# Moving the weight sums of a two-MoE kernel: three steps per piece, other places in the order, and an earlier gather of the inputs of phase one

## Chip, cores and metric

One core of one Trainium2 chip runs the whole kernel in one launch. The metric is the device time of one execution in microseconds; for the kernel before it is 1974.27 us, the median of three runs (1972.3, 1974.27 and 1975.72).

## What is computed

A windowed attention is followed by two mixture-of-experts layers, each with 8 experts on 2304 tokens of width 512, hidden width 1024. The first MoE gives each token to one expert (288 tokens each); the second applies every expert to every token and weighs the results by a matrix P that is balanced in 8 rounds.

```python
def _moe2_ref(x, w_gate, w1, w2):
    logits = x @ w_gate
    P = np.exp(logits - logits.max())
    for _ in range(8):
        P /= P.sum(1, keepdims=True) + 1e-09
        P /= P.sum(0, keepdims=True) + 1e-09
        P *= N / E
    for e in range(E):
        out += P[:, e:e + 1] * (np.maximum(x @ w1[e], 0.0) @ w2[e])
```

## The kernel before

**Number format.** Each fp32 operand is held as two f16 parts, hi and lo, and a product is three matmuls (hi by hi, hi by lo, lo by hi).

**Stages.** Up to about 165 us the attention runs. From there to 747 us, stage 1 (`stage1`) interleaves the router of the first MoE, its eight experts in phases 0 to 7 (`moe1`, after `moe1_x` has transposed the gathered inputs), and expert 0 of the second MoE (`m2_l1(j)`, `m2_l2(j)`: layers 1 and 2 on the j-th of nine column blocks). The end of stage 1, 668.6 to 746.0 us, is `last()`: both layers on blocks 7 and 8, interleaved with a side generator `sinkhorn`, which computes the gate's logits (L1131, L1132: 18 tiles) and balances P (eight rounds, each with a matmul L1157 between two short chains of DVE operations). A side generator goes on whenever the main one has issued as many nanoseconds of matmul as the side asked for in its last `yield`. `drain=False` leaves the rest of `sinkhorn` to the next stage.

**Stage 2** (`stage2`, 747 us to the end) runs experts 1 to 7, each over three blocks of 384 token pairs (below n = 0, 1, 2). It uses Strassen's scheme: seven products of matrix halves instead of eight. `s_l1` issues 28 products (q, i) of six matmuls (L1022, 168 in all), of which `after` makes hidden values: C[i] in a tile "r" of two buffers and S[i] in a tile "S" of one. `split` turns them into f16: hh (ACT, L978) and hl (DVE, L979); its four steps per i are put off over later products by the list `todo`. `s_l2` has 84 steps and 252 matmuls (L1060); `add` sums the products (L1083 to L1093) and weighs them by P into `acc` (L1070).

**Weight sums.** For Strassen each expert's weights are seven sums and pieces of matrix quarters. They come in eight pieces p0 to p7 (four of layer 1, four of layer 2) by the generator `pieces`. For each it loads the raw fp32 weights (SP queue, L903 or L906), makes four sums (DVE, L918 to L921 or L924 to L927; below A), the hi part (ACT, two L937; B) and the lo part (DVE, two L940; C). For experts 2 to 7 both parts go to DRAM (`ws`, POOL queue, L943), and `w_load` brings back a layer's weights whole (SP queue, w1h, w1l, w2h, w2l: 1792 KB each). A piece is done in one go: A and B in one step at one of the steps j = 8, 20, 32, ... of `s_l2`, C and the stores twelve steps on. Expert 1's pieces stay in SBUF: six fall into `last()`, a step every five of its main steps, two into the first `s_l1`. The 18 rows of `acc`, which expert 0 has filled (L880), are scaled by P on POOL (L1288).

**Phase 0.** `weights(("a", 0))` gathers the weights of the first expert through the POOL queue (L768, four tiles of w1a, converted by ACT L747 and DVE); `gather_x` gathers the 288 tokens (L777, three). `moe1_x` transposes them on PE (L809, copied by ACT L810), and `moe1` multiplies (L796).

What sets the order of each engine is the order of these calls in the program; tiles with few buffers add waits.

Of the kernel before, what the change touches and what calls it, by code (L numbers as in the profile page):

```python
# [650 lines left out]
BLK = 384  # L651
# [24 lines left out]
class Moe:  # L676
# [40 lines left out]
    def weights(self, key, letter, fetch):  # L717
# [17 lines left out]
        for it in todo[:4]:  # L735
            load(it)
# [154 lines left out]
    def pieces(self, e, lay, sums, ns=range(4), stored=False):  # L891

        nc = self.nc
        V = nc.vector
        sw = (SW1, SW2)[lay]
# [13 lines left out]
        ns = list(ns)  # L909
        nxt = load(ns[0])  # L910
        yield
        for n in ns:
            r = nxt
            t = sums()
            x = [r[:, k] for k in range(4)]
            if lay == 0:
                a11, a21, a12, a22 = x
                V.tensor_add(t[:, 0], a21, a22)  # L918
                V.tensor_sub(a21, a11, a21)  # L919
                V.tensor_sub(t[:, 1], t[:, 0], a11)  # L920
                V.tensor_sub(t[:, 2], a12, t[:, 1])  # L921
            else:
                b11, b12, b21, b22 = x
                V.tensor_sub(t[:, 0], b12, b11)  # L924
                V.tensor_sub(b12, b22, b12)
                V.tensor_sub(t[:, 1], b22, t[:, 0])
                V.tensor_sub(t[:, 2], b21, t[:, 1])  # L927
            if stored:
                hi, lo = (self.raw.tile([128, 1024], F32, name="raw").bitcast(F16)[:, :7 * 256].rearrange(
                    "p (k c) -> p k c", k=7) for _ in range(2))  # L930
            else:
                hi, lo = (o[:, n] for o in self.wb[lay])
            if n != ns[-1]:
                nxt = load(ns[ns.index(n) + 1])
            parts = (slice(0, 4), r), (slice(4, 7), t)
            for k, x in parts:
                nc.scalar.activation(hi[:, k], x, AF.Copy, scale=sw)  # L937
            yield
            for k, x in parts:
                V.scalar_tensor_tensor(lo[:, k], x, sw, hi[:, k], op0=OP.mult, op1=OP.subtract)  # L940
            if stored:
                for u, x in enumerate((hi, lo)):
                    nc.gpsimd.dma_start(self.ws[lay][u, :, n], x)  # L943
            yield
# [19 lines left out]
    def s_l1(self, b):  # L964
# [16 lines left out]
        def after(q, i):  # L981
# [60 lines left out]
    def s_l2(self, e):  # L1042
# [65 lines left out]
    def load_gate2(self):  # L1108
        nc, sm = self.nc, self.sm
        g = sm.tile([128, KT, E], F32, name="g2f")  # L1110
        self.g2 = sm.tile([128, KT, 2, E], F16, name="g2")
        nc.sync.dma_start(g, self.wg2.rearrange("(k p) e -> p k e", p=128))
        nc.scalar.activation(self.g2[:, :, 0], g, AF.Copy, scale=SG)
        nc.vector.scalar_tensor_tensor(self.g2[:, :, 1], g, SG, self.g2[:, :, 0], op0=OP.mult, op1=OP.subtract)

    def sinkhorn(self):

        nc, sm = self.nc, self.sm
        V = nc.vector
        self.P = P = sm.tile([128, NT, E], F32, name="P")  # L1120
        one_f = sm.tile([128, 128], F32, name="one_p")
        V.memset(one_f, 1.0)
        p = self.r.psum()
        pv = p[:, :2 * NT * E].rearrange("p (t w e) -> p t w e", e=E, w=2)
        for t in range(NT):
            if t % 3 == 0:
                yield 600
            s, j = divmod(t, NT // 2)
            c = slice(128 * j, 128 * (j + 1))
            for k in range(KT):  # L1130
                nc.tensor.matmul(pv[:, t], self.x2[0][:, k, s, c], self.g2[:, k], start=(k == 0), stop=False)  # L1131
# [36 lines left out]
    def stage1(self, ctx):  # L1168
# [30 lines left out]
        def main():  # L1199
# [10 lines left out]
            for ph in range(E):  # L1210
# [16 lines left out]
                if ph + 1 == E:  # L1227
                    break
# [118 lines left out]
```

## Time and profile before

| what | value |
|---|---|
| median of three runs | 1974.27 us |
| profiled execution, its own time | 1982.54 us |
| its span, first to last instruction | 1980.8 us |
| mean granted TensorE clock in it | 0.961 |
| PE busy | 1805.1 us, 91% |
| DVE busy | 1409.7 us, 71% |
| ACT busy | 886.5 us, 45% |
| POOL busy | 322.5 us, 16% |

Rows of a timeline have the start in us, the duration in us, engine, line, operation, tiles written and read, shape and count; what stands in brackets at the end is how long the engine sat idle before the row, and what released it. Rows of waits have the waiting engine's tile and line, the releasing engine's tile and line, the idle time in us, how often, and the longest. PE is TensorE's matmuls, DVE VectorE, ACT ScalarE, POOL GpSimd, SP SyncE (a queue of transfers here).

### The profile page before, as it was taken

The numbers are of one execution on the slowest core, as the hardware profiler recorded it, in microseconds if no ns is written. First come the engines' busy times: TensorE is split into PE (matmuls) and PEld (weight loads), VectorE is DVE, ScalarE is ACT, GpSimd is POOL, SyncE is SP. The second block draws the span as 40 slices with busy tenths as digits, with TensorE's granted clock in tenths as the row PEclk, the third lists the DMA queues.
The fourth block names the chain that finished last, engine by engine and source line by source line (L and its number), as shares of the span: only waits on it lengthen the run. The fifth ranks groups of instructions, "written<-read, shape, count | busy, mean of one in ns | idle before, by whom it ended". The sixth has DMA issues, their size and how long they took to land.

```text
span 1980.8 us, 36661 instructions
## 1 busy us (share of the span) xinstructions
PE 1805.1 (91%) x15082; PEld 1322.0 (67%) x15082; DVE 1409.7 (71%) x2680; ACT 886.5 (45%) x1532; POOL 322.5 (16%) x377
## 2 busy tenths in 40 slices
PE   6997589998899778999999999999999999999998
PEld 4775367665667645677776667777667776766776
DVE  5996677766764377777778777677867777787655
ACT  6784233323334224443454444345544444554333
POOL 0582332222242006000000000000000000000111
PEclk7897699999999889999999999999999999999999
DMA  9275553444463231235333333443334334323220
GB/s 216 68 156 139 108 110 72 99 117 68 110 146 98 69 110 58 98 144 195 137 124 135 136 119 144 161 172 115 124 125 152 144 152 169 127 110 136 89 89 33
DMA packets 139816, 241.21 MB, mean 122 GB/s; under 512 B 74208, under 2 KB 107232, under 8 KB 132736
## 3 DMA queue, kind: packets, MB, share of 16 engines
q1 hardware_dynamic: 118384, 151.25, 23.5%
q0 software_dynamic: 20592, 87.53, 15.3%
q8 instruction: 118, 1.93, 0.4%
q14 instruction: 50, 0.41, 0.1%
q10 hardware_dynamic: 672, 0.08, 0.0%
HBM read 173.74 MB, written 61.74 MB: 119 GB/s over the span
## 4 chain that ended last, share of the span: by engine, by line
issue 49%; PE 6%; POOL 4%; DVE 3%; ACT 1%; DMA 1%; POOLq 0%; SPq 0%; ACTq 0%; DVEq 0%
PE mm L1022 4%; POOL ws L943 2%; POOL acc L1288 2%; PE mm L1060 1%; POOL out_dram L1074 1%; PE mm L877 1%; DMA raw<-in_w2b_dram 1%; DVE raw L940 1%; ACT hh L978 0%; ACT raw L937 0%; DVE hl L979 0%; DVE w1l L940 0%; DVE w2l L940 0%; DVE t L1088 0%; DVE t L1090 0%
## 5 line engine op out<-in xcount | busy, mean ns | idle before, releaser
L1022 PE MATMUL mm<-xb,w1h 128*128 128x384 f16 x2352 | 574.6, 327 | 32.1 <-DVE r L997 26.8
L1060 PE MATMUL mm<-w2h,hh 128*128 128x256 f16 x1764 | 481.4, 273 | 25.5 <-DVE t L1084 12.2
L1060 PE MATMUL mm<-w2l,hh 128*128 128x256 f16 x1764 | 481.5, 273 | 0.0
L1060 PE MATMUL mm<-w2h,hl 128*128 128x256 f16 x1764 | 481.5, 273 | 0.0
L1060 PEld LDWEIGHTS <-hh 128*128 128x128 f16 x3528 | 345.5, 98 | 74.9 <-issue 32.5
L1022 PE MATMUL mm<-xb,w1l 128*128 128x384 f16 x1176 | 384.1, 327 | 0.0
L1022 PEld LDWEIGHTS <-w1h 128*128 128x128 f16 x2352 | 230.3, 98 | 190.5 <-issue 43.7
L943 POOL DMA_DIRECT2D ws<-raw x96 | 51.9, 541 | 965.9 <-ACT raw L937 485.5
L979 DVE TENSOR_TENSOR hl<-r,hh 128x1536 f16<-128x1536 f32 x84 | 147.7, 1758 | 57.1 <-ACT hh L978 57.1
L1060 PEld LDWEIGHTS <-hl 128*128 128x128 f16 x1764 | 172.7, 98 | 20.3
L974 ACT ACTIVATE r<-mm 128x384 f32<-128x384 f32 x252 | 119.0, 481 | 111.2 <-PE mm L1022 111.2
L1022 PEld LDWEIGHTS <-w1l 128*128 128x128 f16 x1176 | 115.2, 98 | 76.4 <-issue 0.5
L978 ACT ACTIVATE hh<-r 128x1536 f16<-128x1536 f32 x84 | 124.6, 1484 | 47.3 <-DVE r L1003 45.2
L937 ACT ACTIVATE raw<-raw 128x1024 f16<-128x1024 f32 x48 | 50.7, 1057 | 203.4 <-DVE raw L919 99.5
L979 DVE TENSOR_TENSOR hl<-S,hh 128x1152 f16<-128x1152 f32 x84 | 113.9, 1356 | 34.5 <-ACT hh L978 34.5
L1070 DVE SCALAR_TENSOR_TENSOR acc<-t,P,acc 128x512 f32<-128x512 f32 x126 | 94.7, 752 | 5.1
L796 PE MATMUL mm<-xt,w1h 128*128 128x288 f16 x512 | 96.9, 289 | 1.6 <-ACT xt L810 1.6
L799 ACT ACTIVATE w1h<-mm 128x288 f16<-128x288 f32 (+1 forms) x120 | 46.9, 396 | 111.2 <-PE mm L796 103.2
L978 ACT ACTIVATE hh<-S 128x1152 f16<-128x1152 f32 x84 | 96.4, 1147 | 0.0
L796 PE MATMUL mm<-x2l,w0h 128*128 128x256 f16 x288 | 82.7, 287 | 10.2 <-DVE x2l L838 10.2
L800 DVE SCALAR_TENSOR_TENSOR w1l<-mm,w1h 128x288 f16<-128x288 f32 (+1 forms) x120 | 50.8, 435 | 49.8 <-ACT w1h L799 45.5
L985 ACT ACTIVATE mm<-mm 128x384 f32<-128x384 f32 x84 | 40.3, 479 | 102.5 <-PE mm L1022 102.5
(287 smaller groups left out, 3313.2 us busy)
## 6 DMA issues: line engine op xcount, KB each, us to landing
ws<-raw POOLq DMA_DIRECT2D x96, 448.0 KB
xb<-xw SPq DMA_DIRECT2D x30, 1344.0 KB
raw<-in_w2b_dram SPq DMA_DIRECT2D x32, 512.0 KB
raw<-in_w1b_dram SPq DMA_DIRECT2D x56, 256.0 KB
w1h<-ws SPq DMA_DIRECT2D x6, 1792.0 KB
w1l<-ws SPq DMA_DIRECT2D x6, 1792.0 KB
w2h<-ws SPq DMA_DIRECT2D x6, 1792.0 KB
w2l<-ws SPq DMA_DIRECT2D x6, 1792.0 KB
```

The costliest lines, as they stand in the source:

```text
L796: nc.tensor.matmul(p, a[:, k, 128 * f:128 * (f + 1)], rhs(k, b), start=(k == 0 and i == 0), stop=(k == KT - 1 and i == 2))
L799: nc.scalar.activation(h[0][:, f, :n], p, AF.Relu)
L800: nc.vector.scalar_tensor_tensor(h[1][:, f, :n], p, 0.0, h[0][:, f, :n], op0=OP.max, op1=OP.subtract)
L937: nc.scalar.activation(hi[:, k], x, AF.Copy, scale=sw)
L943: nc.gpsimd.dma_start(self.ws[lay][u, :, n], x)
L974: nc.scalar.activation(o, p, AF.Relu, scale=SH)
L978: yield nc.scalar.activation(hq[0][:, i, k], x, AF.Copy)
L979: yield V.tensor_sub(hq[1][:, i, k], x, hq[0][:, i, k])
L985: nc.scalar.activation(Q[i], P[i], AF.Copy)
L1022: nc.tensor.matmul(p, w[u][:, 2 * j + i // 2, k, 128 * (i % 2):128 * (i % 2 + 1)], x[:, v, r, j], start=(q in (1, 5) and j == 0 and n == 0 ...
L1060: nc.tensor.matmul(p, h[u][:, i, a, 128 * t:128 * (t + 1)], w[v][:, i, b, :], start=(q in (1, 7) and i == 0 and j == 0), stop=(q in (2, 3) ...
L1070: V.scalar_tensor_tensor(self.acc[:, r, :], x, self.P[:, r, e:e + 1], self.acc[:, r, :], op0=OP.mult, op1=OP.add)
```

## The change

- `pieces` goes. In its place `staged` makes the pieces of experts 2 to 7 in three steps: A; B with the store of hi; C with the store of lo. The lo part is written into a buffer of the tile "r" that C[i] uses. The steps stand at j = 0, 1, 3 of `s_l1` for n = 1 and 2 (p2, p5), and at j = 8, 10, 16 and 20, 23, 43 of `s_l2` (p0, p1 for n = 0; p3, p4 for n = 1; p6, p7 for n = 2). The first raw load is now issued before the first `s_l1` of an expert.
- `direct` makes expert 1's pieces in two steps each (A with B; C): its first loads at step 16 of the last phase's `moe1`, four steps at 40, 44, 52, 56, eight in `last()` at every tenth step, four in the first `s_l1` at j = 7, 13, 19, 25.
- The gate's logits are made after each phase (`gate2(ph - 1)`), two tiles at a time; four of the 18 tiles stay in `sinkhorn`. Its `yield`s become 2000, 1800 and 6000 instead of 1500, 1200 and 3600, and each round has one DVE operation less.
- `acc` is scaled by P on ACT in expert 1's `s_l2`, two rows of 512 ahead of each t's first sum; L1288 goes.
- In `s_l1` the split of the last but one i begins one product later.
- In phase 0 the first two weight gathers come before the tokens', the other two behind them.

The diff, cut to its core:

```diff
         for it in todo[:4]:          # weights()
+        (two loads, a yield, two loads)
 ...
+    def staged(self, e, part):
+        nxt = self.loader(e, 0)(0)
+        yield
+        for i, (lay, n) in enumerate(todo):
+            r = nxt
+            t, lo = part()
+            hi = self.raw.tile([128, 1024], F32, name="raw").bitcast(F16)[:, :7 * 256].rearrange(
+            self.w_sums(lay, r, t)
+            if i + 1 < len(todo):
+                nxt = self.loader(e, todo[i + 1][0])(todo[i + 1][1])
+            split = self.w_split(lay, r, t, hi, lo)
+            next(split)
+            yield
+            next(split)
+            nc.gpsimd.dma_start(self.ws[lay][0, :, n], hi)
+            yield
+            next(split, None)
+            nc.gpsimd.dma_start(self.ws[lay][1, :, n], lo)
+            yield
 ...
-                todo.extend((early, late, None, late))
+                todo.extend((None, early, late, late) if i + 2 == FT // 2 else (early, late, None, late))
 ...
             if q == 2:
+                for r in (row(t, 0), row(t, 1)) if e == 1 else ():
+                    nc.scalar.activation(self.acc[:, r, :], self.acc[:, r, :], AF.Copy, scale=self.P[:, r, 0:1])
 ...
-            yield 3600
+            yield 6000
 ...
-            V.tensor_scalar(cs, cs, float(CAP), None, op0=OP.mult)
 ...
+        self.ready = self.direct(1)
+                    if ph + 1 == E and i in (16, 40, 44, 52, 56):
+                        next(self.ready)
+                if ph:
+                    self.gate2(ph - 1)
 ...
-                    if j % 5 == 0:
-                        next(nxt, None)
+                    if j % 10 == 4 and n:
+                        next(self.ready)
+                        n -= 1
 ...
+        def part():
+            lo = self.tp.tile([128, 2, 2, BLK], F32, name="r", bufs=2).bitcast(F16).rearrange(
+            return self.tp.tile([128, 3, BLK], F32, name="S", bufs=1)[:, :, :256], lo
+        def l1(e, n, b):
+            for j, ns in enumerate(self.s_l1(b)):
+                if (e, n) == (1, 0) and j % 6 == 1 and j > 2:
+                    next(self.ready, None)
+                if n and e + 1 < E and j in (0, 1, 3):
+                    next(new)
+                yield ns
-        for t in range(NT):
-            self.nc.gpsimd.tensor_scalar(self.acc[:, t, :], self.acc[:, t, :], self.P[:, t, 0:1], None, op0=OP.mult)
 ...
-                    if j % 12 == 8:
+                    if j in (8, 10, 16, 20, 23, 43):
                         next(new, None)
```

**DVE at the end of a steady `s_l1`** (a block of stage 2; r, S, hh, hl and mm as above; L997 of before is L1032 after, L979 is L1014). Before:

```order
L993 TENSOR_TENSOR mm<-mm,t_10890 128x384
L1007 TENSOR_TENSOR S<-r,S 128x384
L979 TENSOR_TENSOR hl<-r,hh 128x1536
L997 TENSOR_TENSOR r<-mm,t_10890 128x384
L979 TENSOR_TENSOR hl<-S,hh 128x1152
```

After:

```order
L1028 TENSOR_TENSOR mm<-mm,t_13870 128x384
L1042 TENSOR_TENSOR S<-r,S 128x384
L1032 TENSOR_TENSOR r<-mm,t_13870 128x384
L1014 TENSOR_TENSOR hl<-r,hh 128x1536
L1014 TENSOR_TENSOR hl<-S,hh 128x1152
```

The sum of the last i's bank (r<-mm) now stands ahead of the lo part of C of the last but one i (hl<-r).

**SP at the change from stage 1 to stage 2** (xw: x's Strassen sums, written to DRAM; xb: one block of them read back; raw: weights). Before:

```order
L858 DMA xw_3240<-w2h 128x8x144
L858 DMA xw_3240<-w2l 128x8x144
L862 DMA xw_3240<-x2h 128x2x384 x3
L862 DMA xw_3240<-x2l 128x2x384 x3
L903 DMA raw<-in_w1b_dram 128x2x256 x8
L906 DMA raw<-in_w2b_dram 128x2x512 x2
L1165 DMA oidx<-lst 128x18x1
L953 DMA xb<-xw_3238 128x5376 x2
L906 DMA raw<-in_w2b_dram 128x2x512 x2
```

After:

```order
L903 DMA raw<-in_w1b_dram 128x2x256 x8
L861 DMA xw_3240<-w2h 128x8x144
L861 DMA xw_3240<-w2l 128x8x144
L865 DMA xw_3240<-x2h 128x2x384 x3
L865 DMA xw_3240<-x2l 128x2x384 x3
L906 DMA raw<-in_w2b_dram 128x2x512 x4
L988 DMA xb<-xw_3238 128x5376 x2
```

Expert 1's loads of layer 1 moved ahead of the last stores of xw, and all four of layer 2 ahead of the load of the first xb.

**POOL's queue in phase 0** (widx and idx: lists of gathered rows). Before:

```order
L768 DMA raw<-in_w1a_dram,widx 128x1024 x4
L777 DMA xg<-xd,idx 96x1024 x3
L768 DMA raw<-in_w2a_dram,widx 128x512 x8
```

After:

```order
L771 DMA raw<-in_w1a_dram,widx 128x1024 x2
L780 DMA xg<-xd,idx 96x1024 x3
L771 DMA raw<-in_w1a_dram,widx 128x1024 x2
L771 DMA raw<-in_w2a_dram,widx 128x512 x8
```

The three token gathers stand before the third and fourth weight gather.

## Rows read from the trace of the kernel before

**Rows 1.** The waits of PE, longest sums first: waiting tile and line, releaser; us in all, times, longest.

```profile
PE mm L1022 <- DVE r L997: 26.8, 22, 1.4
...
PE mm L1060 <- DVE t L1084: 12.2, 10, 2.4
PE mm L1060 <- DVE t L1088: 12.2, 18, 1.3
PE mm L809 <- DMA xg<-xd,idx: 11.1, 1, 11.1
...
PE mm L796 <- DVE x2l L838: 10.2, 9, 3.3
PE r L1140 <- DVE mx L1137: 9.4, 1, 9.4
```

**Rows 2.** DVE's timeline at the end of the `s_l1` that began at 1628.8 us.

```profile
1654.44 1.76 DVE L979 TENSOR_TENSOR hl<-r,hh 128x1536 f16<-128x1536 f32 x1 [0.68 <-ACT hh L978]
1656.11 0.55 DVE L997 TENSOR_TENSOR r<-mm,t 128x384 f32<-128x384 f32 x1
```

**Rows 3.** PE's timeline at the same place.

```profile
1656.71 0.49 PE L1022 MATMUL mm<-xb,w1h 128*128 128x384 f16 x2 [1.25 <-DVE r L997]
```

**Rows 4.** DVE's timeline in the `s_l2` that follows (n = 0 of expert 6): the last split, then A and C of a piece.

```profile
1664.21 1.35 DVE L979 TENSOR_TENSOR hl<-S,hh 128x1152 f16<-128x1152 f32 x1
1669.34 0.42 DVE L918 TENSOR_TENSOR S<-raw 128x256 f32<-128x256 f32 x1 [3.78 <-DMA raw<-in_w1b_dram]
...
1671.35 1.23 DVE L940 SCALAR_TENSOR_TENSOR raw<-raw 128x1024 f16<-128x1024 f32 x1 [0.33 <-ACT raw L937]
1672.49 0.95 DVE L940 SCALAR_TENSOR_TENSOR raw<-S,raw 128x768 f16<-128x768 f32 x1
```

**Rows 5.** ACT's timeline there: B of the same piece.

```profile
1670.26 1.06 ACT L937 ACTIVATE raw<-raw 128x1024 f16<-128x1024 f32 x1 [6.70 <-DVE raw L919]
1671.22 0.83 ACT L937 ACTIVATE raw<-S 128x768 f16<-128x768 f32 x1
```

**Rows 6.** Line 1060 in two blocks: a block of expert 7, which has no pieces, and the block of rows 4. Duration in ns (least, median, most), first and last start in us.

```profile
L1060 PE MATMUL mm<-w2h,hh x84: 272/273/273, 1832.2 to 1859.4; 128*128 128x256 f16 x84
```

```profile
L1060 PE MATMUL mm<-w2h,hh x84: 269/273/273, 1657.7 to 1687.7; 128*128 128x256 f16 x84
```

**Rows 7.** The chain that ended last, by time, in the last block (n = 2) of expert 6: start, us, what.

```profile
1774.91 12.96 DMA raw<-in_w2b_dram
```

**Rows 8.** PE's timeline in `last()`: its four long gaps; and the longest gap of the first `s_l1` of stage 2.

```profile
687.67 0.37 PE L1140 MATMUL r<-idf,mx 128*1 128x128 f32 x1 [9.41 <-DVE mx L1137]
...
705.59 0.85 PE L1157 MATMUL r<-P,one_p 128*128 128x144 f32 x2 [6.00 <-DVE P L1154]
...
719.14 0.48 PE L1157 MATMUL r<-P,one_p 128*128 128x144 f32 x2 [2.24 <-DVE P L1154]
...
727.54 0.48 PE L1157 MATMUL r<-P,one_p 128*128 128x144 f32 x2 [4.03 <-DVE P L1154]
...
771.51 0.48 PE L1022 MATMUL mm<-xb,w1h 128*128 128x384 f16 x2 [3.12 <-DVE mm L993]
```

**Rows 9.** Stretches of `last()`: from and to, us, busy us (instructions) of PE, PEld, DVE, ACT and POOL, granted clock, DMA share, GB/s.

```profile
668.60:746.00 77.40, 54.91 (x454) 36.55 (x452) 49.39 (x141) 18.95 (x36) 2.19 (x2) 0.87 0.37 114
680.40:690.70 10.30, 2.93 (x13) 1.73 (x13) 6.56 (x15) 4.78 (x9) 0.00 (x0) 0.50 0.31 99
704.30:711.20 6.90, 5.61 (x26) 4.09 (x27) 6.49 (x20) 0.74 (x3) 0.00 (x0) 0.51 0.41 79
728.20:731.60 3.40, 3.40 (x10) 1.18 (x8) 2.07 (x9) 0.00 (x0) 0.00 (x0) 0.51 0.00 0
```

**Rows 10.** SP's timeline in `last()`: loads of raw weights and of the first xb (the duration covers the issue of all transfers of the row).

```profile
676.46 17.58 SPq L903 DMA_DIRECT2D raw<-in_w1b_dram  x8
...
715.64 0.81 SPq L953 DMA_DIRECT2D xb<-xw  x2
```

**Rows 11.** DVE's timeline where it waits for the first of them.

```profile
681.30 0.42 DVE L918 TENSOR_TENSOR raw<-raw 128x256 f32<-128x256 f32 x1 [9.58 <-DMA raw<-in_w1b_dram]
```

**Rows 12.** PE's timeline: the first three gate tiles of `sinkhorn` and what follows them (24 matmuls, three tiles, up to the second row).

```profile
669.58 0.17 PE L1131 MATMUL r<-g,x2h 128*128 128x16 f16 x1
...
670.18 0.27 PE L796 MATMUL mm<-x2h,w0h 128*128 128x256 f16 x1
```

**Rows 13.** Line 880, ACT's copy of a 512-wide row of `acc`: ns, first and last start.

```profile
L880 ACT ACTIVATE acc<-mm x18: 597/597/617, 297.4 to 746.0; 128x512 f32<-128x512 f32 x18
```

**Rows 14.** ACT's timeline in phase 0: the conversion of the fourth weight tile, then the copies of the transposed tokens.

```profile
232.99 1.06 ACT L747 ACTIVATE w1h<-raw 128x1024 f16<-128x1024 f32 x1 [6.57 <-DMA raw<-in_w1a_dram,widx]
234.31 1.73 ACT L810 ACTIVATE xt<-mm 128x768 f16<-128x768 f16 x2 [0.27 <-PE mm L809]
```

**Rows 15.** POOL's timeline: one store of weight sums (448 KB), whose bytes rows 16 show as they move.

```profile
1791.02 0.54 POOL L943 DMA_DIRECT2D ws<-raw  x1 [4.22 <-ACT t L1083]
```

**Rows 16.** Stretches of 1 us behind that store, columns as in rows 9.

```profile
1791.50:1792.50 1.00, 0.99 (x10) 0.89 (x10) 1.00 (x3) 0.05 (x1) 0.06 (x1) 1.00 0.46 186
1792.50:1793.50 1.00, 1.00 (x12) 0.90 (x10) 1.00 (x2) 0.38 (x1) 0.00 (x0) 1.00 0.68 272
```

**Rows 17.** Line 1022 in the `s_l1` of rows 2, columns as in rows 6.

```profile
L1022 PE MATMUL mm<-xb,w1h x112: 323/326/327, 1628.8 to 1657.4; 128*128 128x384 f16 x112
```

**Rows 18.** ACT's timeline in it: the first write of C[1].

```profile
1640.66 0.47 ACT L974 ACTIVATE r<-mm 128x384 f32<-128x384 f32 x1
```

More of the change, by code (lines that the diff above doesn't have):

```diff
@@ L733, in load @@
             live.append((it, r))
-        for it in todo[:4]:
+        for it in todo[:2]:
+            load(it)
+        yield
+        for it in todo[2:4]:
             load(it)
@@ L889, with loader @@
     RIGHT1 = {1: 0, 2: 1, 3: 2, 4: 6, 5: 3, 6: 4, 7: 5}
-    def pieces(self, e, lay, sums, ns=range(4), stored=False):
+    def loader(self, e, lay):
         nc = self.nc
-        V = nc.vector
-        sw = (SW1, SW2)[lay]
         w = self.w["b"][lay][e]
@@ L907, in load @@
             return r
-        ns = list(ns)
-        nxt = load(ns[0])
-        yield
-        for n in ns:
-            r = nxt
[L914 to L937, printed above, removed]
-            yield
[L939 to L943, printed above, removed]
@@ new lines, in loader, with w_sums @@
+        return load
+    def w_sums(self, lay, r, t):
+        V = self.nc.vector
+        x = [r[:, k] for k in range(4)]
+        if lay == 0:
+            a11, a21, a12, a22 = x
+            V.tensor_add(t[:, 0], a21, a22)
+            V.tensor_sub(a21, a11, a21)
+            V.tensor_sub(t[:, 1], t[:, 0], a11)
+            V.tensor_sub(t[:, 2], a12, t[:, 1])
+        else:
+            b11, b12, b21, b22 = x
+            V.tensor_sub(t[:, 0], b12, b11)
+            V.tensor_sub(b12, b22, b12)
+            V.tensor_sub(t[:, 1], b22, t[:, 0])
+            V.tensor_sub(t[:, 2], b21, t[:, 1])
@@ new lines, in w_split, with direct @@
+    def w_split(self, lay, r, t, hi, lo):
+        sw = (SW1, SW2)[lay]
+        parts = (slice(0, 4), r), (slice(4, 7), t)
+        yield
+        for k, x in parts:
+            self.nc.scalar.activation(hi[:, k], x, AF.Copy, scale=sw)
+        yield
+        for k, x in parts:
+            self.nc.vector.scalar_tensor_tensor(lo[:, k], x, sw, hi[:, k], op0=OP.mult, op1=OP.subtract)
+    def direct(self, e):
+        todo = [(lay, n) for lay in range(2) for n in range(4)]
+        live = [self.loader(e, lay)(n) for lay, n in todo[:2]]
+        yield
+        for i, (lay, n) in enumerate(todo):
+            r = live.pop(0)
+            t = self.raw.tile([128, 4, 256], F32, name="raw")[:, :3]
+            self.w_sums(lay, r, t)
+            split = self.w_split(lay, r, t, *(o[:, n] for o in self.wb[lay]))
+            next(split)
+            next(split)
+            yield
+            next(split, None)
+            if i + 2 < len(todo):
+                lay, n = todo[i + 2]
+                live.append(self.loader(e, lay)(n))
+            yield
@@ L1193, in fetched @@
             next(w)
+            if ph:
+                next(w)
             self.gather_x(ph)
+            if not ph:
+                next(w)
             return w
         first = fetched(0)
+        self.ready = self.direct(1)
         def main():
@@ L1242, in stage1 @@
         interleave(main(), side, lambda: SLACK if self.ph == 1 else SL2)
-        def sums():
-            return self.raw.tile([128, 4, 256], F32, name="raw")[:, :3]
         def last():
@@ L1274, in stage2 @@
             self.warm(1)
-        rest = self.pieces(1, 1, lambda: self.raw.tile([128, 4, 256], F32, name="raw")[:, :3], range(2, 4))
-        def first():
-            for j, ns in enumerate(self.s_l1(0)):
-                if j % 4 == 0:
-                    next(rest, None)
-                yield ns
-        next(rest)
-        interleave(first(), self.side)
-        for _ in rest:
-            pass
-        for t in range(NT):
-            self.nc.gpsimd.tensor_scalar(self.acc[:, t, :], self.acc[:, t, :], self.P[:, t, 0:1], None, op0=OP.mult)
         for e in range(1, E):
             order = list(range(NB))[::1 if e % 2 else -1]
-            new = [self.pieces(e + 1, lay, sums, stored=True) for lay in range(2)] if e + 1 < E else []
-            new = itertools.chain(*new)
+            new = self.staged(e + 1, part) if e + 1 < E else iter(())
             for n, b in enumerate(order):
-                if (e, n) != (1, 0):
-                    for _ in self.s_l1(b):
+                if n == 0:
+                    next(new, None)
+                interleave(l1(e, n, b), self.side if (e, n) == (1, 0) else None)
+                if (e, n) == (1, 0):
+                    for _ in self.ready:
                         pass
```

57 lines of the change are left out of this document (35 added, 22 removed).

## Prediction

> **What bounds the kernel now.** The waits of PE come first [rows 1], because PE is busy for nine tenths of the span: only time that PE stands still, or runs at half clock, can come back. The largest sum is 26.8 us in 22 equal waits at one line of `s_l1`. Two sums of 12.2 us lie in `s_l2`, on the sums that DVE makes of the products. Then come single waits: 11.1 us for the first tokens, 9.4 us in `last()`. The timelines tell what DVE did meanwhile, the stretches tell the clock. The reader should see that DVE, busy 71% of the span, is no bound on average; it is late at a few places, where long operations of the weight sums or of the split stand ahead of a short one that PE needs. The chain that ended last agrees at one place: a load of raw weights of 12.96 us [rows 7].
>
> All sums are against the profiled execution, 1982.54 us; the median, 1974.27 us, is 0.4% lower, and I subtract the same microseconds from it. A difference under 0.2%, 4 us, can't be told from none.
>
> **Part 1, the end of `s_l1`.** Before, DVE did 1.76 us of hl<-r and then the 0.55 us sum [rows 2] for which PE stood 1.25 us [rows 3]. The new order puts the sum first, and the 1.76 us behind it. PE's product before the gap ended at 1655.46 (1656.71 - 1.25); with hl<-r out of its way the sum ends, by my replay of the order, at about 1655.0, so some 0.4 us before PE asks for it. Next late would be hl<-r, by 0.55 us, and its first reader is the second half of the `s_l2` that follows; nobody waits for it there. Twenty blocks (all but the first) x 1.25 = **25.0 us**. Bounds: 15, if half a microsecond stays in each, and 26.8, the whole of the wait.
>
> **Part 2, `s_l2`.** The floor is the block without pieces: 1832.2 to 1859.4 from first to last product; the n = 0 block of expert 6 takes 30.0 against 27.2 [rows 6]. In it DVE waits 3.78 us for the raw weights [rows 4], so A (1.67 us, four sums), B (1.06 + 0.83 on ACT [rows 5]) and C (1.23 + 0.95 [rows 4]) fall on the time in which the first sums of t are due. Afterwards the first load is issued a block earlier. The split ends 7.9 us into the block (1664.21 + 1.35 - 1657.7); A ends at 9.6, B at 11.5, C or the second piece's A by 13.7, and PE first needs a sum of t at its 49th of 84 steps, 48/84 of 27.5 = 15.7 us. So the gaps of the n = 0 blocks of experts 2 to 6 go: I add them up to 9.6 of the 24.4 us in [rows 1]. **+9.6**, bounds 0 (the second load is late again) and 11. In n = 1 one piece fewer is in the way: +1.3. In n = 2 nothing is won: the load of rows 7 still stands on SP behind the 3.6 MB of w1h and w1l, and the last steps wait for it; the hi part's store, now sent ahead of the lo part's, competes with that load. I take -2 over six blocks, bounds -6 and +4.
>
> **Part 3, expert 1's first blocks.** The 18 scalings of `acc` leave POOL, which nobody waited for, and come to ACT, ahead of the copies that PE waits for: 18 x 0.60 us, priced by a row of the same size [rows 13], = 10.8 us, hidden where ACT has room. Bounds 0 and -10.8. Each pair delays one copy by 1.2 us, and only the first t's is asked for at once: I take about a third, -4. The first `s_l1` loses its long gap [rows 8], but gets two weight pieces and about three of the eight rounds of balancing; DVE has more there than before, and I replay it to **-1** (bounds -6, +4).
>
> **Part 4, `last()`.** It takes 77.4 us [rows 9]. The four gaps of [rows 8] and one of 0.77 are 22.45 us of it. The first comes from a load that SP issued only at 676.46 [rows 10], behind the stores of xw: DVE waited 9.58 us for it [rows 11], with the balancing queued behind on the same engine. The others are rounds of balancing whose DVE operations stand behind a piece's A and C (3.85 us). In the three stretches at a clock of 0.50 or 0.51, the lower level of 1.2 GHz, PE is busy 2.93 + 5.61 + 3.40 us, half of which is lost: 5.97. Two of them follow or hold the gaps of 9.41 and 6.00 us. The change loads expert 1's weights in the last phase already, does two of the pieces there, spaces rounds at 6 us instead of 3.6, and moves 14 of 18 gate tiles (0.60 us for three [rows 12], 2.8 us) into the phases. What is left is 77.4 - 22.45 - 5.97 - 2.8 = 46.2. DVE's work in it falls from 49.4 to about 36 us (two pieces at 3.85, three rounds at some 2). With 3 us of new stalls it takes 49: **+28**. Bounds: 18, if gaps of the size of the last two and one dip of the clock stay, and 31. The gate tiles go where PE waits for x2l, 10.2 us in nine waits [rows 1]: 0, bounds -3 and +1. The price at the end: the load of xb now stands on SP behind a raw load that waits for a free buffer, and so for the piece before it. The last stores of xw, now behind eight loads, belong to the block that is read third: free. By the order the xb lands 45 to 48 us into `last()`, as long as that takes: -1.5, bounds -3 and 0.
>
> **Part 5, phase 0.** PE waited 11.1 us for the tokens [rows 1]. They would be issued about 2.5 us earlier. But the first product also needs ACT to convert four weight tiles, and the fourth's conversion at 232.99 stood ahead of the tokens' copies at 234.31 [rows 14]. That tile's gather is now behind the tokens', while the conversion still stands ahead of the copies. **-1**, bounds -5 and +2.
>
> The sum: 25.0 + 9.6 + 1.3 - 2 - 4 - 1 + 28 - 1.5 - 1 = **54.4 us**, 1928 us for the profiled execution and **1920 us** for the median.
>
> **A rule against it.** A store of 448 KB, issued at 1791.02, moved 186 and 272 KB in the stretches that end at 1792.5 and 1793.5, while DVE was busy for all of both [rows 15, 16]; it was through 2.5 us after its issue. The Trainium skill ("SBUF — State Buffer", "SBUF: two separate sides", the trap that DVE blocks DMA) says that a transfer issued on POOL's queue can starve, because its descriptors cannot be written while DVE holds the port that both share. The row doesn't bear it out at this place, and by the row the sum stays as it is. By the rule the stores, now put beside the busiest stretches of DVE, would come late, and the time would be that of the fourth rival.
>
> **Rivals.**
>
> 1. *The balancing still stalls PE.* The rounds and the pieces stay on one in-order DVE; a piece's A and C ahead of a round delay it by 3.85 us. For it: just this happened three times [rows 8]. Against it: 6 us between rounds, a third of DVE's time free. Then `last()` gives 18 instead of 28: 1930 us.
> 2. *Another wait takes the place of the one at the end of `s_l1`.* The last sums need banks that ACT frees, and the split's lo part now comes later. For it: the margin is only some 0.4 us. Without the 25.0: 1945 us.
> 3. *Loads, not steps, set `s_l2`.* Two raw loads still pass through SP behind 2.7 MB of xb. For it: the releaser in [rows 4] is a DMA, and so is rows 7. Without 9.6 and with -2 more: 1932 us.
> 4. *Slower: the lo part's store holds a buffer of "r".* C[1] takes the buffer from which p2's and p5's lo part is being stored, in 12 blocks (n = 1 and 2 of experts 1 to 6). Its first write was due 11.9 us into the block [rows 17, 18]; by my replay the store is issued 7.2 us into it, and PE stands only from 14.5 us, when a product needs the bank that waits. So the store may take 7.3 us, where one took 2.5 [rows 15, 16]. Each microsecond beyond costs 12. It turns the result when a store takes 7.3 + 54.4/12 = 11.8 us; at 13 the time is 1974.3 - 54.4 + 12 x 5.7 = 1988 us.
>
> **How the numbers follow.** Forecast 0.55: the gaps are named by rows, each with the work ahead of it moved. Rival 1 has 0.2, since DVE's order there was only replayed; rival 3 0.1, rival 2 0.08, rival 4 0.05; 0.02 for no change in the queues that are waited for. With the upper bounds of the largest two gains, parts 2 and 4, and nothing lost in parts 3 and 5, 70 us would come back: 1904, the lower end. Rivals 1 and 3 lie inside, and the upper end reaches to rival 2: 1904 to 1946. Faster by over 0.2% in all but rival 4 and the leftover: 0.93; within 0.2% 0.02; slower 0.05.
>
> **What would show it.** Right: the wait of L1022 on the sum falls from 26.8 to under 3 us; a block of `s_l1` takes 27.6 us where it took 28.9 (1628.8 [rows 17] to 1657.7 [rows 6]); the waits on L1084 and L1088 fall from 24.4 to about 15 with what is left in n = 2; the stretch from gate to stage 2 is 49 us with no gap over 3 us, and its clock near 1. Wrong: PE waits in early `s_l1` released by ACT's write of r, which itself waited for a DMA (rival 4); a clock of 0.5 inside `last()` (rival 1); a new releaser at the end of `s_l1` (rival 2); raw loads as releasers in n = 0 (rival 3). A result above 1946 us would make the forecast wrong in its largest part.

## The result, and the profile after

The changed kernel takes **1919.81 us** (median of four runs, 1918.72 to 1923.02) against 1974.99 us before (1972.3 to 1979.77): a ratio of 0.9721, 95% interval 0.9698 to 0.9743. The forecast was 1920. The profiled execution went from 1982.54 to 1918.72 us and its span from 1980.8 to 1916.8, so by 64 us, since that of before was 8 us above its median and that of after was not. The parts are measured against these 64 us.

The waits of PE, as in [rows 1]:

```profile
PE mm L1095 <- DVE t L1121: 12.2, 8, 2.9
...
PE mm L799 <- DVE x2l L841: 8.1, 7, 3.3
...
PE mm L812 <- DMA xg<-xd,idx: 4.8, 2, 3.4
PE mm L1057 <- DVE mm L1028: 4.7, 3, 2.4
PE mm L799 <- ACT xt L813: 4.7, 1, 4.7
...
PE mm L1095 <- DVE t L1125: 4.0, 3, 1.3
```

The row of 26.8 us is gone: nothing of `s_l1` waits for the counterpart of L997 (now L1032). L1121 and L1125 are L1084 and L1088 of before: 16.2 us where they had 24.4.

DVE at the end of a steady `s_l1`, as in [rows 2]:

```profile
1657.77 0.56 DVE L1032 TENSOR_TENSOR r<-mm,t 128x384 f32<-128x384 f32 x1 [0.77 <-PE mm L1057]
1658.24 1.75 DVE L1014 TENSOR_TENSOR hl<-r,hh 128x1536 f16<-128x1536 f32 x1
```

The sum now waits for PE, not PE for it; the long hl<-r follows.

A block of `s_l1` and the `s_l2` behind it (n = 0 of expert 6), as in [rows 17, 6]:

```profile
L1057 PE MATMUL mm<-xb,w1h x112: 322/326/326, 1577.0 to 1604.2; 128*128 128x384 f16 x112
```

```profile
L1095 PE MATMUL mm<-w2h,hh x84: 272/273/273, 1604.5 to 1631.7; 128*128 128x256 f16 x84
```

The n = 0 block runs from 1604.5 to 1631.7, as long as a block without pieces. From first product to the next block's first product, in us, each block from one trace (of the 20 steady `s_l1` one took 29.01 before and one 27.62 after):

| kernel | `s_l1`, steady | `s_l2` n = 0, experts 2 to 6 | n = 1, the same | n = 2, the same | expert 1: first `s_l1`; `s_l2` n = 0, 1, 2 |
|---|---|---|---|---|---|
| before | 28.89 | 29.41 to 30.67 | 28.15 to 28.16 | 28.38 to 31.54 | 36.44; 31.21, 28.31, 29.56 |
| changed | 27.48 | 27.51 | 27.51 | 28.39 to 30.07 | 36.56; 30.51, 30.26, 32.45 |

What stays in n = 2 is the load of [rows 7]. The chain that ended last there has it with nearly the same length, and on DVE the sums of p7 wait for it:

```profile
1715.62 12.54 DMA raw<-in_w2b_dram
```

```profile
1728.26 0.43 DVE L922 TENSOR_TENSOR S<-raw 128x256 f32<-128x256 f32 x1 [1.91 <-DMA raw<-in_w2b_dram]
```

The end of stage 1 takes 52.7 us instead of 77.4 [rows 9]. Columns as there:

```profile
671.70:724.40 52.70, 47.51 (x338) 32.19 (x336) 37.04 (x104) 17.57 (x38) 0.00 (x0) 0.94 0.44 137
676.00:684.00 8.00, 6.04 (x52) 4.54 (x53) 5.26 (x20) 2.91 (x8) 0.00 (x0) 0.57 0.69 188
```

The four gaps of [rows 8] in it are gone; PE waits for no round of balancing. But new gaps have come at its start, and the clock fell once more, to 0.57 on average in 676 to 684 us. PE there, and DVE:

```profile
673.15 0.18 PE L1162 MATMUL r<-g,x2h 128*128 128x16 f16 x1 [0.98 <-ACT x2h L840]
...
676.67 0.19 PE L1163 MATMUL r<-g,x2l 128*128 128x8 f16 x1 [2.23 <-DVE x2l L841]
...
678.36 0.17 PE L1162 MATMUL r<-g,x2h 128*128 128x16 f16 x1 [1.29 <-DVE P L1166]
```

```profile
674.16 2.09 DVE L935 SCALAR_TENSOR_TENSOR w1l<-raw,w1h 128x1024 f16<-128x1024 f32 x2
676.16 0.45 DVE L841 SCALAR_TENSOR_TENSOR x2l<-mm,x2h 128x288 f16<-128x288 f32 x1
```

The second of expert 1's pieces, which the change moved into the last phase, stands with its lo part of 2.09 us ahead of the last x2l, for which PE waits 2.23 us; all gaps from 672 to 678.4 us are 5.2 us.

### The profile page after: what moved, and what is told of

The parts are those of the page before. It is cut to its first block, busy times and chain, and to the rows that moved or that the text cites. A ratio compares the mean times of both kernels' runs of the same rounds, so it can differ in the third digit from the quotient of the medians.

```text
span 1916.8 us, 36731 instructions
## 1 busy us (share of the span) xinstructions
PE 1796.9 (94%) x15082; PEld 1321.2 (69%) x15082; DVE 1415.7 (74%) x2681; ACT 894.9 (47%) x1558; POOL 286.7 (15%) x359
## 4 chain that ended last, share of the span: by engine, by line
PE 60%; DVE 14%; issue 11%; DMA 7%; ACT 5%; POOL 2%; another core or an unknown queue 0%; SPq 0%; POOLq 0%; DVEq 0%; ACTq 0%
PE mm L1057 24%; PE mm L1095 18%; PE mm L799 8%; PE mm L880 4%; DMA raw<-in_w2b_dram 4%; PE mm L836 2%; DMA rawq<-in_q_dram 1%; DVE nm L230 1%; DMA raw<-in_w2a_dram,widx 1%; DVE w1l L751 1%; PE r L552 1%; POOL out_dram L1109 1%; ACT raw L932 1%; DVE hl L1014 1%; DVE ptl L256 1%
## 5 line engine op out<-in xcount | busy, mean ns | idle before, releaser
L1014 DVE TENSOR_TENSOR hl<-r,hh 128x1536 f16<-128x1536 f32 x84 | 147.5, 1755 | 41.2 <-ACT hh L1013 41.2
L975 POOL DMA_DIRECT2D ws<-raw x48 | 25.9, 540 | 952.2 <-ACT raw L932 769.0
L1014 DVE TENSOR_TENSOR hl<-S,hh 128x1152 f16<-128x1152 f32 x84 | 113.5, 1352 | 0.0
```

Source lines behind the costliest of these rows:

```text
L1014: yield V.tensor_sub(hq[1][:, i, k], x, hq[0][:, i, k])
```

## Experiments

Medians are of several runs, each beside runs of the kernel before on the same chip, whose own medians were 1979 to 1985 us; blocks are read from one trace of each kernel, as in the table above. The medians of the kernel before, here and in the result, differ by up to 10 us between chips (1974.99 and 1985.38), so edits worth less are judged by their blocks.

| kernel | median, us | ratio to before, 95% interval |
|---|---|---|
| todo_only | 1955.1 | 0.9857, 0.9838 to 0.9876 |
| load_late | 1949.1 | 0.9845, 0.9825 to 0.9865 |
| p7_early | 1905.99 | 0.9631, 0.9615 to 0.9647 |
| lo_slow | 1931.09 | 0.9750, 0.9729 to 0.9771 |
| acc_mid | 1913.85 | 0.9665, 0.9649 to 0.9681 |
| acc_q6 | 1914.67 | 0.9645, 0.9596 to 0.9694 |
| early_pieces | 1925.98 | 0.9717, 0.9698 to 0.9736 |
| no_early_pieces | 1918.12 | 0.9685, 0.9669 to 0.9701 |
| one_early | 1919.14 | 0.9665, 0.9630 to 0.9699 |
| dense_rounds | 1930.1 | 0.9729, 0.9692 to 0.9766 |
| x_late | 1920.15 | 0.9698, 0.9682 to 0.9714 |
| combined | 1902.95 | 0.9581, 0.9545 to 0.9618 |

**1. The order at the end of `s_l1`, alone.**

```diff
 # before.py
-                todo.extend((early, late, None, late))
+                todo.extend((None, early, late, late) if i + 2 == FT // 2 else (early, late, None, late))
```

> The kernel before with nothing but the later start of the split of the last but one i in s_l1. Theory (the end of s_l1 is a matter of this order alone): the 20 steady blocks of s_l1 fall from 28.89 to 27.5 us, s_l2 stays as it was (28.2 to 31.5), so -28 us: about 1946 us. Rival A (the blocks also needed the weight sums moved): less than 10 us come back, over 1964 us. Rival B (hl<-r, now later, delays the head of s_l2): s_l2 grows by what s_l1 wins, 1974 us.

The steady blocks take 27.48 us (one 27.51), and `s_l2` of experts 1 to 6 stays at 28.16 to 31.55. Its waits, and a block:

```profile
PE mm L1022 <- DVE r L997: 0.4, 1, 0.4
```

```profile
L1022 PE MATMUL mm<-xb,w1h x112: 323/326/326, 1613.8 to 1640.9; 128*128 128x384 f16 x112
```

So one line gives 20 x 1.41 = 28.2 us, and the ratio, 1.4% of 1982, says the same. Rivals A and B are out.

**2. The lead of the first load.**

```diff
 # after.py
-                if n == 0:
-                    next(new, None)
                 interleave(l1(e, n, b), ...)
 ...
                     self.x_load(order[n + 1])
+                    if n == 0:
+                        next(new, None)
```

> The changed kernel, but each expert's first raw load is issued behind its first s_l1, as before, and not ahead of it; the three steps stay where they are. Theory (the load's lead wins the n = 0 blocks of s_l2): the first sum waits until about 11.7 us into s_l2, PE waits for t again, the five n = 0 blocks of experts 2 to 6 take 29 to 30.5 us where they take 27.51 now: +8 to +14 us, 1928 to 1934 us. Rival (the split into three steps wins them): they stay within 0.3 us of 27.51, 1920 us.

The n = 0 blocks of experts 2 to 6 take 30.37 to 33.90 us, 24.4 more in all than in the changed kernel and 11.5 more than before, and expert 1's 4.0 more than in the changed kernel. DVE in the block of expert 6, which began at 1626.0:

```profile
1636.86 0.43 DVE L916 TENSOR_TENSOR S<-raw 128x256 f32<-128x256 f32 x1 [3.21 <-DMA raw<-in_w1b_dram]
...
1640.99 0.43 DVE L916 TENSOR_TENSOR S<-raw 128x256 f32<-128x256 f32 x1
...
1644.06 1.09 DVE L1121 TENSOR_TENSOR t<-mm,t 128x256 f32<-128x256 f32 x3 [1.38 <-ACT t L1120]
```

Two pieces' sums (1636.86 and 1640.99) now stand ahead of the first sum of t, where the old places had one, and PE's waits come as one gap of 2.7 to 3.7 us. Expert 6's block, the shortest, is as long as before (30.37 us and 30.34); the other four are 2.0 to 3.4 us longer, and there the granted clock fell behind the gap. PE in the block of expert 2, which began at 939.7, and the two blocks whole, columns as in [rows 9]:

```profile
959.31 0.37 PE L1095 MATMUL mm<-w2h,hh 128*128 128x256 f16 x1 [3.73 <-DVE t L1121]
```

```profile
939.70:973.60 33.90, 30.17 (x254) 25.95 (x253) 23.71 (x39) 9.25 (x15) 2.16 (x4) 0.90 0.54 198
1626.00:1656.30 30.30, 27.60 (x253) 24.58 (x252) 23.46 (x39) 9.21 (x15) 2.16 (x4) 1.00 0.60 221
```

So with the steps at their new places the lead wins these blocks, and these steps with a late load do harm. The size was missed by a factor of about two because the gap came in one piece and the clock fell with it. The lead with the steps at their old places was not tried.

**3. The last load ahead of the big ones.**

```diff
 # after.py, staged(); r is taken from a list of loaded pieces
             nc.gpsimd.dma_start(self.ws[lay][1, :, n], lo)
+            if i == 5:
+                live.append(self.loader(e, 1)(3))
             yield
```

> The changed kernel, but the load of the last piece p7 is issued behind the third step of p5, in the first third of the last s_l1 of an expert, and so ahead of the loads of w1h and w1l on SP. Theory (in n = 2 the step that makes p7's sums waits for this load, and the sums of t behind it): the n = 2 blocks of experts 2 to 6 fall from 28.4 to 30.1 to under 28 us, expert 1's by 2: -7 to -10 us, 1910 to 1913 us. Rival (the late step is late by DVE's own work, or the w1h and w1l loads then hold up the next s_l1): 1918 to 1922 us.

The n = 2 blocks of experts 2 to 6 take 27.51 us, each of them; that of expert 1 30.22. On SP the load of p7 is now the fourth of a row that stands ahead of w1h, issued at 1704.54:

```profile
1650.68 19.26 SPq L906 DMA_DIRECT2D raw<-in_w2b_dram  x4
...
1704.54 0.34 SPq L985 DMA_DIRECT2D w1h<-ws  x1
```

The sum is 10.6 us by the blocks, and no `s_l1` got longer. So the load, not DVE's work, was the rest in n = 2.

**4. The price of a late store.**

```diff
 # after.py, staged()
+            for s in range(3) if i in (2, 5) else ():
+                nc.gpsimd.dma_start(self.scr[s], lo)
             nc.gpsimd.dma_start(self.ws[lay][1, :, n], lo)
```

> The changed kernel with three more copies of the lo part of p2 and p5 (448 KB each) stored to an unused place in DRAM, ahead of the real store, in the 12 blocks where C[1] takes that buffer next. It doubles and more the time that the store holds the buffer: some 5 us more. Theory (the fourth rival's price: PE stands only from 14.5 us into the block): the first write of C[1] comes at 14 to 17 us instead of 12, the s_l1 blocks with it grow by 0 to 2.5 us, +0 to +30 us. Rival A (PE stands with the write itself, from 12 us): +3 to +5 us in each, +36 to +60 us. Rival B (the four stores move at once and land within the old slack): the blocks stay at 27.48, 1920 us within 3.

Each of the 12 blocks takes 28.70 or 28.71 us, 1.23 more: 14.7 us, and the median is 11 higher. POOL, then ACT, in the block that began at 1643.8:

```profile
1650.83 1.60 POOL L980 DMA_DIRECT2D scr<-r  x3 [1.88 <-DVE r L936]
1652.42 0.54 POOL L981 DMA_DIRECT2D ws<-r  x1
```

```profile
1657.64 0.49 ACT L1012 ACTIVATE r<-mm 128x384 f32<-128x384 f32 x1 [1.88 <-PE mm L1060]
```

The first write of C[1] comes 13.8 us into the block instead of 11.9. The row names a product of PE as what released it; but the bytes of the four stores moved until just before, and in the changed kernel ACT did not wait there. A stretch of 1 us, and PE's longest wait in the block:

```profile
1656.00:1657.00 1.00, 1.00 (x8) 0.61 (x7) 1.00 (x1) 0.00 (x0) 0.00 (x0) 1.00 0.42 172
```

```profile
1663.24 0.48 PE L1060 MATMUL mm<-xb,w1h 128*128 128x384 f16 x2 [0.61 <-DVE mm L1031]
```

In the changed kernel the same write stood at its old place [rows 18], 4.84 us behind the store:

```profile
1639.06 0.54 POOL L978 DMA_DIRECT2D ws<-r  x1 [1.88 <-DVE r L935]
```

```profile
1643.90 0.47 ACT L1009 ACTIVATE r<-mm 128x384 f32<-128x384 f32 x1
```

```profile
1640.00:1641.00 1.00, 1.00 (x9) 0.61 (x7) 0.41 (x1) 0.56 (x2) 0.00 (x0) 1.00 0.90 380
1641.00:1642.00 1.00, 1.00 (x8) 0.61 (x7) 0.96 (x3) 0.01 (x1) 0.00 (x0) 1.00 0.20 79
```

The last view gives stretches of 1 us: the store's 459 KB had moved within 3 us of its issue. The mechanism of the fourth rival exists; it did not act, with some 2 us to spare. But PE has lost 1.2 us already where the write comes at 13.8 us; I had replayed that it stands only from 14.5. It did not stand at the bank that I had named, but 19.4 and 25.8 us into the block, for sums of DVE that had become late in turn.

**5. The scalings of `acc`, at two other places.**

```diff
 # acc_mid: s_l2, the scalings taken out of add()
+            if rows and k >= 20 and k % 4 == 0:
+                r = rows.pop()
+                nc.scalar.activation(self.acc[:, r, :], self.acc[:, r, :], AF.Copy, scale=self.P[:, r, 0:1])
 # acc_q6: add(), out of q == 2 and behind the copy of q == 6
                 nc.scalar.activation(t1[t][:, R], X[t][:, L], AF.Copy)
+                for r in (row(t, 0), row(t, 1)) if e == 1 else ():
+                    nc.scalar.activation(self.acc[:, r, :], self.acc[:, r, :], AF.Copy, scale=self.P[:, r, 0:1])
```

> The changed kernel, but the 18 scalings of acc by P on ACT do not stand ahead of the first sum of each t; they are spread over the steps 20 to 40 of expert 1's s_l2, one every four entries of its order. Theory (part 3 of the prediction: they delay the copies that PE waits for): the three blocks of s_l2 of expert 1 fall from 30.51, 30.26 and 32.45 us to 27.5 to 28.5, 27.5 to 28 and 29 to 30.5: -6 to -8 us, 1912 to 1914 us. Rival (DVE's leftover of the first s_l1 and the pieces hold these blocks up): less than 2 us come back.

The three blocks took 29.91, 29.66 and 34.39 us: 0.7 more in sum than in the changed kernel, as the rival had it in number, but not for its reason. ACT in acc_mid, n = 0:

```profile
774.39 0.83 ACT L932 ACTIVATE raw<-S 128x768 f16<-128x768 f32 x1
775.13 2.54 ACT L1143 ACTIVATE acc<-acc,P 128x512 f32<-128x512 f32 x4
777.58 0.63 ACT L1118 ACTIVATE t<-mm 128x256 f32<-128x256 f32 x2
```

Four scalings had piled up behind a piece's hi part, which waited for its sums, and ran right ahead of the copies. An earlier place in the program is no earlier time on an engine that works in order.

> The changed kernel, but the two scalings of acc by P for each t stand behind the copy for product 6 instead of ahead of the copy for product 2; spreading them over earlier steps only moved the wait (the three blocks of s_l2 of expert 1 took 29.91, 29.66 and 34.39 us instead of 30.51, 30.26 and 32.45). Theory (ACT's order ahead of the first copies is what costs): the gaps before the first product 6 and the first product 4 go, the three blocks fall to 27.5 to 28, 27.5 to 28 and 30 to 30.5 us: -6 to -8 us, 1912 to 1914 us. Rival (DVE's own order is late too, so that the wait comes back at product 4 or 3): -2 us or less, 1918 us or more.

27.62, 27.51 and 31.46 us, 6.6 less than in the changed kernel. The same engine there:

```profile
783.84 0.91 ACT L1118 ACTIVATE t<-mm 128x256 f32<-128x256 f32 x3
786.22 0.38 ACT L1121 ACTIVATE t<-mm 128x256 f32<-128x256 f32 x1 [1.47 <-PE mm L1095]
786.50 1.32 ACT L1123 ACTIVATE acc<-acc,P 128x512 f32<-128x512 f32 x2
```

The copies follow one another, and the scalings stand where ACT waited for PE. What is left in n = 2 is p7's load (experiment 8).

**6. Where expert 1's pieces go.**

```diff
 # early_pieces
-                    if ph + 1 == E and i in (16, 40, 44, 52, 56):
+                    if ph + 1 == E and i in (8, 20, 24, 28, 32):
 # no_early_pieces: i in (16,), twelve steps in last(), at j % 7 == 3
 # one_early: i in (16, 40, 44), ten steps in last(), at j % 8 == 4
 # dense_rounds: the yields of sinkhorn 1500, 1200, 3600
```

> The changed kernel with the five steps of expert 1's pieces in the last phase moved from steps 16, 40, 44, 52, 56 of moe1 to 8, 20, 24, 28, 32, so ahead of the sums of the last x2. Theory (the 5.2 us of gaps at 672 to 678 us and the low clock at 677 to 684 us come from a lo part of 2.09 us that stands on DVE ahead of the last x2l): gaps fall to 2 us or less, the low clock goes, -5 to -8 us: 1912 to 1915 us. Rival (x2l is late by its own chain through ACT, and the gate's tiles ask for it at once): gaps stay, 1920 us within 2.

Inconclusive by its time. These pieces overwrite weights that the last phase's first layer still reads, so that layer works with other data, and the writes wait for its reads; PE waits for them in turn:

```profile
659.45 0.42 PE L799 MATMUL mm<-xt,w1h 128*128 128x288 f16 x2 [3.29 <-ACT w1h L932]
```

The last phase grew from 24.0 to 33.4 us. What follows it, up to stage 2, shrank from 53.9 to 48.5.

> The changed kernel, but the last phase only loads expert 1's first two pieces; the four steps at 40 to 56 go into the end of stage 1, where twelve steps now stand seven main steps apart. Theory (a piece's lo part of 2.09 us on DVE ahead of the last x2l makes PE wait 2.2 us and more at 672 to 678 us, and the low clock at 677 to 684 us follows from that): gaps there fall from 5.2 to 2 to 3 us, the low clock is gone or shorter, and the stretch from 671.7 to stage 2 falls from 53.9 to 46 to 50 us: 1912 to 1917 us. Rival (DVE becomes the bound there, 37 us of work + 7.7 in 46): new gaps before the rounds of balancing or in the first s_l1, 1920 us or up to 1926.

That stretch took 59.8 us: the rival held. PE waits for the rounds again, as in [rows 8]:

```profile
695.99 0.51 PE L1200 MATMUL r<-P,mean 128*128 128x144 f32 x2 [3.13 <-DVE P L1197]
...
706.67 0.48 PE L1200 MATMUL r<-P,mean 128*128 128x144 f32 x2 [1.87 <-DVE P L1197]
```

The gaps at its start fell from 5.2 to 1.3 us, as the theory had it, and 9.6 us of others came. The span is 1922.2 us, 5.4 more than the changed kernel's; the median, from another chip, does not show that, and the profiled execution was the slowest of four (1915.18 to 1923.98).

> The changed kernel with one of expert 1's pieces made in the last phase (steps 16, 40, 44), not two, and ten steps of pieces in the end of stage 1, eight main steps apart. All four taken out of the phase made that end longer, 59.8 us for 53.9, by waits for the rounds of balancing. Theory (both hold: the second piece delays the last x2l, and the end of stage 1 has no more room on DVE than for one piece): gaps at 672 to 678 us fall from 5.2 to 2 to 3 us, and gaps before the rounds of 0 to 3 us appear: the end takes 50 to 54 us, 1916 to 1920 us. Rival (DVE has room for one piece more): 48 to 50 us and no gap before a round, 1914 us. Second rival (it has none): 57 us or more, 1923 us.

52.0 us, with 1.3 us of gaps at the start and 3.8 later: the theory. The lower clock is gone too:

```profile
673.70:724.60 50.90, 45.65 (x342) 30.81 (x340) 37.60 (x105) 16.86 (x36) 0.00 (x0) 1.00 0.49 152
```

With the first `s_l1` at 35.01 and the first `s_l2` at 32.20 it is 1.8 us less than the changed kernel.

> The changed kernel with the distances of the balancing rounds of before (1500, 1200 and 3600 ns of main work instead of 2000, 1800 and 6000). Theory (the spacing is what keeps rounds and pieces apart on DVE): PE waits before rounds again, 2 to 6 us each at two to four of them, the end of stage 1 takes 58 to 66 us, but the first s_l1 has no rounds left and loses its two gaps of 2.4 and 2.1 us: +1 to +8 us in sum, 1921 to 1928 us. Rival (the early loads and the early pieces alone brought the gain of the end of stage 1): 54 us or less there, and the sum 2 to 5 us less, 1915 to 1918 us.

61.4 us, the first `s_l1` 33.58 and the first `s_l2` 32.19: 6.2 more in sum than in the changed kernel, though two gaps of 2.2 and 2.4 us stayed in the first `s_l1`, which the theory had not. Two of the rounds:

```profile
703.36 0.48 PE L1200 MATMUL r<-P,mean 128*128 128x144 f32 x2 [1.89 <-DVE P L1197]
...
714.75 0.48 PE L1200 MATMUL r<-P,mean 128*128 128x144 f32 x2 [1.79 <-DVE P L1197]
```

So of the 24.7 us that the end of stage 1 lost, the spacing accounts for 7.5, which the next blocks give back by 1.3; the rest is left for the early loads with the two early pieces and the gate tiles that left. I did not take these apart.

**7. The tokens' gather.**

```diff
 # x_late: weights() issues four gathers, then gather_x, as before
```

> The changed kernel with the gathers of phase 0 in the order of before (four weight tiles, then the tokens). The trace of the change has its first product of phase 0 at 232.6 us instead of 237.4, but phase 2 begins at 358.1 instead of 357.9. Theory (the router's rounds set the later phases, the 4.8 us are swallowed there): 1920 us, within 3 us. Rival (the gain holds and something else in the phases lost as much): 4 to 6 us slower, 1925 us.

1920.15 us, no difference. Its first product of phase 0 came at 231.91, no later than the changed kernel's 232.60, although the order of the gathers was that of before:

```profile
227.87 0.82 PE L809 MATMUL mm<-id,xg 96*128 96x96 f16 x8 [6.29 <-DMA xg<-xd,idx]
...
231.91 0.64 PE L796 MATMUL mm<-xt,w1h 128*128 128x288 f16 x2 [1.36 <-ACT xt L810]
```

In the changed kernel the tokens came earlier, and PE then waited for their copies on ACT:

```profile
224.44 0.52 PE L812 MATMUL mm<-id,xg 96*128 96x96 f16 x8 [3.38 <-DMA xg<-xd,idx]
...
232.60 0.64 PE L799 MATMUL mm<-xt,w1h 128*128 128x288 f16 x2 [4.68 <-ACT xt L813]
```

ACT there converted the fourth weight tile, whose gather was now the last, ahead of these copies:

```profile
229.40 1.06 ACT L750 ACTIVATE w1h<-raw 128x1024 f16<-128x1024 f32 x1 [0.23 <-DMA raw<-in_w1a_dram,widx]
230.36 2.19 ACT L813 ACTIVATE xt<-mm 128x768 f16<-128x768 f16 x3
```

So the 4.8 us that phase 0 began earlier after the change can't be put down to the order, and neither theory is needed: with the old order, too, phase 0 began anywhere from 231.9 to 240.4 us (x_late and todo_only).

**8. A version that beats both**: p7_early, acc_q6 and one_early together.

> The changed kernel with the three edits that took a wait out: p7's load behind the third step of p5, the scalings of acc behind the copy for product 6, and one of expert 1's pieces instead of two in the last phase. By the blocks of their traces against those of the change: n = 2 of experts 1 to 6 falls by 10.6 us with the first, the blocks of expert 1 by 6.6 with the second, the end of stage 1 and the first two blocks by 1.8 with the third. Theory (the three waits are independent): all 18 blocks of s_l2 of experts 1 to 6 take 27.5 to 28, but for the first (up to 29.5): -17 to -20 us against the change, 1900 to 1903 us. Rival (p7's load and the scalings share the same last wait in n = 2 of expert 1): -15 us, 1905 us.

1902.95 us. All blocks of `s_l2` of experts 1 to 6 take 27.51 to 27.55 us but the first (29.13), and every steady `s_l1` 27.48 but one (27.63). The waits were independent: p7's load and the scalings together took expert 1's n = 2 from 32.45 to 27.51.

## Why the prediction was right, and where it was right by luck

**Part 1** (25.0): right in mechanism, 28.2 measured (experiment 1). That is above the upper bound of 26.8, since the gap of 1.25 us was not the whole: the block fell by 1.41. Where the other 0.16 us went is not shown.

**Part 2** (9.6 + 1.3 - 2): n = 0 gave 12.9, n = 1 3.2 and n = 2 2.4 us, by the blocks of experts 2 to 6. The cause, the lead of the load, is shown for n = 0 (experiment 2). For n = 1 the size was too small: each of the five blocks lost its whole 0.64 us. That p7's load is the rest in n = 2 is shown too (experiment 3). I subtracted 2 for a competing store; no run shows such a price. That n = 2 got shorter instead is not shown to be a gain of the change: 2.4 us lie in expert 3's block alone, 31.54 to 29.18, and there the kernel before had a longer gap at the first sum of t, with the lower clock behind it, in this one trace:

```profile
1267.90 0.37 PE L1060 MATMUL mm<-w2h,hh 128*128 128x256 f16 x1 [2.40 <-DVE t L1084]
```

```profile
1249.60:1281.20 31.60, 29.20 (x255) 25.39 (x253) 23.29 (x38) 9.46 (x15) 2.16 (x4) 0.95 0.50 193
```

The changed kernel's gap there is 1.51 us, its clock 1.00. todo_only, with the weight sums as before, has the five blocks in 146.3 us, the changed kernel in 145.9.

**Part 3** (-4 and -1): the three `s_l2` came out 4.1 us longer. The cause of these is shown: another place for the scalings gives back 6.6 (experiment 5). The first `s_l1` came out 0.1 us longer, not 1 shorter: its gap of 3.12 us is gone, but two of 2.38 and 2.08 us, also for DVE's sums, stand in it now, and the clock is 0.91 where it was 0.95:

```profile
725.60:762.10 36.50, 31.82 (x175) 18.49 (x174) 28.98 (x58) 21.27 (x33) 0.00 (x0) 0.91 0.00 0
```

**Part 4** (28 and -1.5): 24.7, and nothing at the load of xb. The step that failed is the 3 us of new stalls: I looked for them at the rounds, which waited for nobody, and missed that the moved piece stands ahead of the last x2l. There PE had 5.2 us of gaps and, beside them, some 7 of 8 us at the lower clock (0.57 on average). Without that piece (one_early, experiment 6) 1.3 us of the gaps stay, and the lower clock is gone, so the piece is the cause of the rest. But no experiment removed it for nothing: with the piece elsewhere, gaps of 3.8 us came at other places, and the stretch was only 1.9 us shorter.

**Part 5 and the gate** (-1 and 0): no gain from the earlier gather (experiment 7), and the trace has the reason given: a conversion that waits for its gather stands on ACT ahead of the copies. But stage 1's last stretch began 3.1 us later in the changed kernel's trace; 2.8 would be the gate tiles, which I had put into gaps for nothing. This is argued, not shown, since these phases differ by several microseconds between executions of any of these kernels.

The parts, as differences of the two traces, add up to 28.2 + 18.5 - 4.2 + 24.7 - 3.1 = 64.1 us, the difference of the two spans. I forecast 54.4, and the medians differ by 55.2: the agreement to 0.2 us is luck, for what the parts lacked is about what the profiled execution of before stood above its median. The lower end of the range calls parts 2 and 4 the largest two gains; by the sum they are parts 4 and 1. x_late, which differs from the changed kernel by nothing that its trace shows, stood 61.5 us below the kernel before on its own chip.

**The rivals.** Rival 1's sign came, a clock near 0.5 inside `last()`, but not its cause: PE waited for the piece ahead of x2l and for no round, and 24.7 us came back, not 18. It was near, though: by the prediction's own numbers DVE was to be free for a quarter of the time (36 of 49 us busy), not a third, and denser rounds brought its waits back (experiment 6). Rival 2 did not come: no new releaser at the end of `s_l1`. Rival 3 is half true: n = 2 is set by its load. Rival 4 did not act; its price is real, but begins earlier than I said (experiment 4). The Trainium skill's rule on starved descriptors ("SBUF — State Buffer", "SBUF: two separate sides") stood behind it. At this place the store came through within 3 us of its issue, with DVE busy for 0.96 us of the last (experiment 4). That does not test the rule: the section speaks of DVE operations that hold the shared port, with an fp32 `tensor_copy` as its example, and those that ran on DVE from the store's issue until its bytes had moved are all TENSOR_TENSOR.

## What to carry to other kernels

Where PE waits for a short operation, look at what stands ahead of it on its in-order engine: moving one long operation behind it was worth half of the whole change. A load issued earlier and steps put earlier belong together, since these steps with a late load only stood in the way (experiment 2). When work is moved off a busy place, ask for whom it will stand in line at the new one: the pieces ahead of the last x2l and the scalings ahead of the copies each cost some 4 to 7 us.

## What I had not expected of the hardware

The time from the first weight gather to the first product of phase 0 was 25.8 us (206.12 to 231.91, x_late), 30.2 (before) and 31.8 (todo_only) in the three traces with the old order of gathers, and 28.4 to 31.3 in the eleven with the new one: no order of two or three gathers can be judged from one trace.

And the lower of the two clock levels follows short gaps too, but not each time. In the kernel before it stood beside gaps of 4.03 to 9.41 us [rows 8, 9]; in the changed kernel it followed gaps of 5.2 us in total, none over 2.3 (0.57 on average over 8 us). In `s_l2` it followed a single gap of 2.40 us in the kernel before and one of 2.06 in dense_rounds, but not one of 2.40 in the changed kernel. So the same wait can cost a block nearly 2 us more in one trace than in another (n = 2 of expert 5: 31.39 us in dense_rounds with its gap of 2.06, 30.07 in the changed kernel with 2.40), and the price of a wait is better read from several blocks.
